# Banded attention with a gated feed-forward on one core: masks between the value tiles, last Q/K tokens third, global exponentials first, third batch by hardware DMA

## The chip, the core and the metric

The kernel runs on one core of one Trainium2 chip. The core has five engines with instruction streams of their own: TensorE (PE), VectorE (DVE), ScalarE (ACT), GpSimd (POOL) and SyncE (SP, which here only issues DMA transfers). Each engine takes its instructions strictly in the order in which the program gives them; semaphores hold an instruction until its inputs are there and its buffer is free. The metric is the device time of one execution in microseconds (us). Lower is better.

## The reference, cut to what matters

```python
B, H, S, D = 8, 8, 576, 64            # batch, heads, tokens, head size; 8 global tokens
scores = q @ k.T / sqrt(D)
mask = |i - j| <= 32  or  i is global  or  j is global
x = softmax(where(mask, scores, -1e9)) @ v            # then to (4608, 512): tokens x (heads * D)
g, val = x @ w_gate, x @ w_val                        # 512 -> 1536
ffn = (gelu(g) * val) @ w_out                         # 1536 -> 512
out = x + sigmoid(x @ w_res) * ffn
```

Inputs and outputs are fp32; the kernel multiplies in bf16 and accumulates in fp32.

## The kernel before

**Windows and chunks.** Each batch of 576 tokens is cut into 9 windows of 64 queries, each of which sees 128 keys around it. The 72 windows of the 8 batches are taken in 9 chunks of 8 windows (512 tokens): a chunk is the unit of the feed-forward part. `sc` holds the scores of four windows (a *quad*) and two heads; `weigh` (L456) takes the exponential into `pt` on ACT, and one multiplication by `maskw` per bank on DVE (L469) takes away what lies outside the band. So a quad has four exponentials and four masks, and a chunk has two quads. `values` (L484 to L504) makes a *value tile* of two windows: PE multiplies `pt` with the values into the psum tile `nd`, of which there is one buffer, and DVE divides (`rden`, `xtok`). Tiles 0 and 1 use quad 0, tiles 2 and 3 use quad 1. `turn_x` transposes the result into `xt`, by DMA for the first three tiles of chunks 2 to 8 and on PE otherwise.

**Global tokens.** Their Q, K and V rows are gathered by indirect DMA (`gather`, L285), four sets for the eight batches. `global_scores` (L404, L409) multiplies them with all keys and queries of a batch, `global_exp` (L416, L418, L420) takes the exponentials `ptg` and `gt` and masks the second, and `global_rows` (L426) makes the outputs of the global rows in `sn`, which shares the buffer of `nd`.

**Feed-forward.** For each of 12 slices j, `ffn_in` (L522 to L530) makes the gate and value products, GELU on ACT, and their product `ht` on DVE. `ffn_out` gives four jobs for each 128 tokens t: the residual gate (`r_ps` L539, tanh L542) and three *thirds* of the output product (`f_ps`, L549). The last third adds `prb` on DVE (L553), `ob` on POOL (L555) and the store on SP (L557). `prb` and `ob` have two buffers each.

**Order.** There is no scheduler: the order is written out by hand. While chunk c goes through `ffn_out`, the scores and values of chunk c+1 stand between its 16 jobs; a table `jobs` says what goes ahead of which. For chunks 1 to 7:

```python
jobs[0].append(lambda: global_exp(b, *held))
jobs[4].append(lambda: global_rows(b))
for quad in range(2):
    jobs[1 + 4 * quad].append(lambda quad=quad: scores(c + 1, quad))
for t in range(4):
    jobs[5 + 2 * t].append(lambda t=t: values(c + 1, t))
    jobs[7 + 2 * t].insert(0, lambda t=t: turn_x(c + 1, t))
```

The end of chunk 0 has an order of its own (L690 and after), since there batch 1 has just come in.

**Psum.** `psm` has four banks (products, part of the scores), `pss` two (the other scores, transposes), `psn` one double bank (`sg`, `sn`, `nd`).

**Loads.** The first two batches come as fp32 by hardware DMA on SP (`load_raw` L159, `load_vraw` L177), as do the weights in 20 pieces of 512 KB (`load_piece` L134). They land in staging room, part of which are buffers that are not yet in use, and are cast by POOL, DVE or ACT (`cast_pair` L253, `cast_v` L182, `cast_piece` L137). `q_st` and `k_st` hold Q and K of one batch in bf16 by tokens; `turn_pair` transposes them on PE for the first two batches, `turn_qk` (L398) by DMA for the others, whose loads (`load_qk` L91, `load_v` L99) are casting DMA transfers that POOL issues. `shift_v` copies the values shifted by 64 tokens from `ve` to `vo`.

Of the kernel before, what the change touches and what calls it, by code (L numbers as in the profile page):

```python
# [23 lines left out]
def kernel(  # L24
# [12 lines left out]
    nc = tc.nc  # L37
# [124 lines left out]
    for p in (0, 1, 2, 3, -1):  # L162
        load_raw(0, "k", p, nc.sync)
        if p == 0:
            nc.scalar.dma_start(gi8, bass.AP(tensor=g32.tensor, offset=g32.offset, ap=[[2, NG], [1, 2]]))
        load_raw(0, "q", p, nc.scalar if p in (0, 1) else nc.sync)
# [13 lines left out]
    def cast_v(b, c, copy):  # L180
        for p0, p1 in ((32, 64), (64, 128)) if c == 0 and b else ((0, 96 if c == 4 else 128),):
            copy(ve[b][p0:p1, c, :, 0:D], vplace[b][c][p0:p1, :].rearrange("p (h d) -> p h d", d=D))  # L182

# [275 lines left out]
    def scores(c, quad):  # L459
# [7 lines left out]
        for pp, u, sc in banks:  # L467
            mine = weigh(quad, pp, u, sc)
            nc.vector.tensor_tensor(mine, mine, view(maskw, 0, 128, 64 * i0, [[0, 2], [64, 4], [1, 64]]), ALU.mult)  # L469
# [94 lines left out]
    for p, by in ((0, (DVE, ACT)), (1, (DVE, ACT)), (2, (POOL, POOL)), (3, (POOL, POOL)), (-1, (POOL, ACT))):  # L564
        if p == 1:
            first_masks()
        for what, copy in zip("kq", by):
            cast_pair(0, p, what, copy)
        if p == 0:
            nc.scalar.activation(far, iota_f, ACTF.Square, bias=ngp, scale=1.0)  # L570
    for what in "kq":
        turn_pair(0, 0, what)
    hot_rows(0)
# [3 lines left out]
    first_scores(0, 0)  # L577
    for what in "kq":
        turn_pair(0, 2, what)
# [7 lines left out]
    for what in "kq":  # L587
        turn_pair(0, -1, what)
    sg, ss = global_scores(0)
    first_scores(0, 1)  # L590
    nc.vector.scalar_tensor_tensor(maskg, far, 1024.5, nong, ALU.is_gt, ALU.mult)
    fill(blk, 1.0, [([[-8, 16]], 1, 0, ALU.is_ge, 0.0), ([[8, 16]], -1, 7, ALU.is_ge, 0.0)])
    global_exp(0, sg, ss)
    nc.vector.tensor_tensor(diag, blk[:, 0:8], blk[:, 8:16], ALU.add)
# [31 lines left out]
    for c in range(NCH):  # L626
        b = c + 1
        if b < B and c:
            turn_qk(b)
            if c == 1:  # L630
# [3 lines left out]
            load_v(b)  # L634
        held = None
        for j in range(NFF):
            ffn_in(c, j)
            if c == 0:
# [14 lines left out]
                elif j == 5:  # L653
# [6 lines left out]
                    for n in (14, 15, 16, 17):  # L660
                        load_piece(n)
                    for n in (12, 13):
                        cast_piece(n, POOL)
                        load_piece(n + 6)
                    for c5 in range(5):
                        cast_v(1, c5, POOL)
                    for n in range(14, 20):
# [4 lines left out]
            elif b < B:  # L672
                if c == 1:
                    if j == 8:
                        double_qk(1, B // 2)
                    elif j == 9:
                        got = turn_globals(1, B // 2)
                        for what in "kq":
                            DVE(compact[what][:, 1:B // 2, :], got[what])
                        spread_v(1, B // 2)  # L680
# [10 lines left out]
        if c == 0:  # L691
            held = global_scores(1)
            work_f[0]()
            global_exp(1, *held)
            shift_v(1, nc.scalar)
            scores(1, 0)
            work_f[4]()
            scores(1, 1)
            work_f[8]()
            work_f[12]()  # L700
            global_rows(1)
            for i, n in enumerate((1, 5, 2, 6, 3, 7, 9, 10, 11, 13, 14, 15)):
                work_f[n]()
                if i < 4:
                    values(1, i)
                if 1 < i < 6:
                    turn_x(1, i - 2)
                if i == 3:
                    load_qk(2)
                    for what in "kqv":  # L710
                        gather(what, 1)
            continue
        jobs = {n: [] for n in range(16)}
        if c + 1 < NCH:
            if held is not None:
                jobs[0].append(lambda: global_exp(b, *held))
                jobs[4].append(lambda: global_rows(b))
            for quad in range(2):
                jobs[1 + 4 * quad].append(lambda quad=quad: scores(c + 1, quad))
            for t in range(4):  # L720
                jobs[5 + 2 * t].append(lambda t=t: values(c + 1, t))
                jobs[7 + 2 * t].insert(0, lambda t=t: turn_x(c + 1, t))
        for n in range(16):
# [32 lines left out]
```

## Time and profile before

| | |
|---|---|
| median of 9 runs | 425.27 us (424.11 to 426.23) |
| the profiled execution | 425.4 us; span from first to last instruction 423.7 us |
| busy, share of the span | PE 92%, DVE 48%, POOL 41%, ACT 40% |
| mean granted TensorE clock | 0.994 |
| start, to the first gate product of chunk 0 | 0 to 34.75 us |
| chunk 0, gate and value products | 34.75 to 59.69 us |
| chunk 0, output part (with batch 1's first scores) | 59.69 to 85.67 us |
| chunk 1 | 85.67 to 129.79 us |
| chunk 2 | 129.79 to 172.57 us |

Times in the table's lower half are positions in the profiled execution. An instruction's idle time is that of its engine just before it, and the arrow behind it names what ended that idle time. Where several things were waited for, only the one that came last is named. The clock row says at what share of full speed TensorE was let run.

### The profile page before, as it was taken

How to read it: one execution, taken by the hardware profiler on the slowest of the kernel's cores; microseconds unless marked ns; L12 is line 12 of the kernel's file. 1: busy time of each engine (PE TensorE's matmuls, PEld its weight loads, DVE VectorE, ACT ScalarE, POOL GpSimd, SP SyncE). 2: the span in 40 equal slices, each digit the busy share in tenths (PEclk: the TensorE clock that was granted, in tenths of full speed). 3: DMA queues.
4: the chain of work that ended last, by engine and by line, in shares of the span. 5: the costliest groups of instructions: out<-in, count | busy, mean ns of one | idle time of the engine just before them, and what ended most of it. 6: DMA issues, size and time to landing. Idle time of an engine off the chain costs nothing.

```text
span 423.7 us, 7941 instructions
## 1 busy us (share of the span) xinstructions
PE 388.4 (92%) x3084; PEld 203.9 (48%) x3136; DVE 203.0 (48%) x414; ACT 168.7 (40%) x279; POOL 172.9 (41%) x208
## 2 busy tenths in 40 slices
PE   3478979999989999999899999998999999989995
PEld 2354445544554455445544554455445544544442
DVE  6455635535663455346534654365435543463321
ACT  4555556023524362435243523352335233614320
POOL 7688769379316621644165316431600120012012
PEclk9999998999999999999999999999999999999999
DMA  8999979149937993799379926993592230031001
GB/s 245 236 389 336 236 262 137 57 115 129 156 86 102 173 108 80 103 152 135 76 102 157 135 76 96 170 127 74 93 140 53 70 68 0 2 89 51 0 26 75
DMA packets 151830, 52.10 MB, mean 123 GB/s; under 512 B 136368, under 2 KB 140976, under 8 KB 151792
## 3 DMA queue, kind: packets, MB, share of 16 engines
q0 software_dynamic: 84768, 11.02, 41.6%
q1 hardware_dynamic: 66304, 39.52, 39.9%
q10 hardware_dynamic: 720, 1.06, 0.9%
q8 instruction: 24, 0.39, 0.4%
q14 instruction: 14, 0.11, 0.1%
HBM read 39.19 MB, written 9.44 MB: 115 GB/s over the span
## 4 chain that ended last, share of the span: by engine, by line
PE 55%; issue 27%; POOL 5%; ACT 4%; DMA 4%; DVE 3%; POOLq 0%; ACTq 0%; DVEq 0%
PE v_ps L526 15%; PE g_ps L522 14%; PE f_ps L549 11%; PE r_ps L539 4%; POOL ob L555 4%; DMA ht<-in_q_dram 3%; PE nd L490 2%; ACT pt L456 2%; PE sg L404 2%; PE nd L484 1%; PE sn L426 1%; PE sc L449 1%; DVE xtok L504 1%; DMA out_dram<-ob 1%; PE ss L409 1%
## 5 line engine op out<-in xcount | busy, mean ns | idle before, releaser
L555 POOL TENSOR_TENSOR ob<-prb,xtok 128x512 f32<-128x512 f32 x36 | 41.5, 1153 | 201.6 <-DVE prb L553 201.6
L530 DVE SCALAR_TENSOR_TENSOR ht<-gsb,v_ps 128x512 bf16<-128x512 bf16 x108 | 74.0, 687 | 99.7 <-PE v_ps L526 93.1
L529 ACT ACTIVATE gsb<-g_ps 128x512 bf16<-128x512 f32 x108 | 64.4, 597 | 137.2 <-PE g_ps L522 126.7
L526 PE MATMUL v_ps<-xt,wv_t 128*128 128x512 bf16 x431 | 110.8, 379 | 1.4 <-DVE ht L530 0.9
L522 PE MATMUL g_ps<-xt,wg_t 128*128 128x512 bf16 x415 | 108.5, 379 | 1.2 <-ACT xt L515 0.7
L549 PE MATMUL f_ps<-wo_t,ht 128*128 128x512 bf16 x413 | 99.8, 379 | 0.9
L526 PEld LDWEIGHTS <-wv_t 128*128 128x128 bf16 x432 | 42.2, 98 | 52.1 <-issue 1.2
L522 PEld LDWEIGHTS <-wg_t 128*128 128x128 bf16 x432 | 42.0, 98 | 50.4 <-issue 0.8
L549 PEld LDWEIGHTS <-ht 128*128 128x128 bf16 x432 | 39.2, 98 | 39.8
L542 ACT ACTIVATE rsb<-r_ps 128x512 bf16<-128x512 f32 x36 | 21.5, 599 | 87.9 <-PE r_ps L539 86.7
L553 DVE SCALAR_TENSOR_TENSOR prb<-rsb,f_ps 128x512 f32<-128x512 bf16 x36 | 24.7, 687 | 32.1 <-PE f_ps L549 29.5
L456 ACT ACTIVATE pt<-sc 128x512 bf16<-128x512 f32 x72 | 37.4, 609 | 3.1 <-PE sc L449 3.0
L539 PE MATMUL r_ps<-wr_t,xt 128*128 128x512 bf16 x129 | 36.8, 388 | 0.7
L469 DVE TENSOR_TENSOR pt<-pt,maskw 128x512 bf16<-128x512 bf16 x64 | 27.8, 438 | 17.8 <-ACT pt L456 14.9
L91 POOL DMA_DIRECT2D q_st<-in_q_dram x30 | 25.4, 870 | 22.5 <-DMA qt<-q_st 22.5
L91 POOL DMA_DIRECT2D k_st<-in_k_dram x30 | 25.5, 878 | 5.3 <-DMA kt<-k_st 4.1
L99 POOL DMA_DIRECT2D ve<-in_v_dram x30 | 25.5, 866 | 0.0
L504 DVE TENSOR_TENSOR xtok<-nd,rden 128x512 bf16<-128x512 f32 x34 | 23.5, 691 | 1.3
L484 PE MATMUL nd<-vgs,gt 128*128 128x260 bf16 x80 | 15.0, 277 | 9.0 <-DVE xtok L504 6.6
L490 PEld LDWEIGHTS <-pt 128*128 128x128 bf16 x576 | 22.2, 97 | 1.1
L490 PE MATMUL nd<-ve,pt 128*128 128x65 bf16 x320 | 22.3, 193 | 0.0
L503 DVE RECIPROCAL rden<-nd 128x8 f32<-128x8 f32 x34 | 7.0, 206 | 29.5 <-PE nd L490 29.3
(134 smaller groups left out, 298.6 us busy)
## 6 DMA issues: line engine op xcount, KB each, us to landing
out_dram<-ob SPq DMA_DIRECT2D x36, 256.0 KB
vo<-ve SPq DMA_DIRECT2D x12, 260.0 KB
q_st<-in_q_dram POOLq DMA_DIRECT2D x24, 128.0 KB, 5.7
k_st<-in_k_dram POOLq DMA_DIRECT2D x24, 128.0 KB, 6.3
ve<-in_v_dram POOLq DMA_DIRECT2D x18, 128.0 KB, 5.9
wo_t<-in_k_dram SPq DMA_DIRECT2D x8, 256.0 KB
extra<-in_moe_w_gate_dram SPq DMA_DIRECT2D x4, 512.0 KB
extra<-in_moe_w_out_dram SPq DMA_DIRECT2D x4, 512.0 KB
```

What stands on the lines that cost most here:

```text
L91: nc.gpsimd.dma_start(dst[0:n, r, :].rearrange("p (h d) -> p h d", d=D), src[b].rearrange("h s d -> s h d")[128 * r:128 * r + n])
L456: nc.scalar.activation(mine, sc, ACTF.Exp, bias=0.0, scale=SCALE)
L469: nc.vector.tensor_tensor(mine, mine, view(maskw, 0, 128, 64 * i0, [[0, 2], [64, 4], [1, 64]]), ALU.mult)
L490: nc.tensor.matmul(nds[h // 4][:, VG * (h % 4):VG * (h % 4) + VG], view(pt, 0, 128, c0, [[1, 128]]), vw, start=False, stop=(h % 4 == 3 and ...
L504: nc.vector.tensor_tensor(xtok[c % 2][:, t, :].rearrange("p (a h d) -> p a h d", a=2, d=D), num[:, :, :, 0:D], view(rden, 0, 128, 0, [[4, ...
L522: nc.tensor.matmul(g_ps, wg_t[:, kk, 128 * j:128 * j + 128], x[:, kk, :], start=(kk == 0), stop=(kk == NKT - 1))
L526: nc.tensor.matmul(v_ps, wv_t[:, kk, 128 * j:128 * j + 128], x[:, kk, :], start=(kk == 0), stop=(kk == NKT - 1))
L529: nc.scalar.activation(gsb, g_ps, ACTF.Gelu, bias=0.0, scale=1.0)
L530: nc.vector.scalar_tensor_tensor(ht[:, j, :], gsb, 0.5, v_ps, ALU.mult, ALU.mult)
L539: nc.tensor.matmul(r_ps, xt[c % 2][:, kk, 128 * t:128 * t + 128], wr_t[:, kk, :], start=(kk == 0), stop=(kk == NKT - 1))
L549: nc.tensor.matmul(held["f"], ht[:, j, 128 * t:128 * t + 128], wo_t[:, j, :], start=(j == 0), stop=(j == NFF - 1))
L555: nc.gpsimd.tensor_tensor(ob, prb, xtok[c % 2][:, t, :], ALU.add)
```

## The change

Four things are moved or replaced; the computation stays.

1. `scores` no longer emits the masks; it returns a function that does. In chunks 1 to 7, value tile 0 stands ahead of the second quad's scores, two of that quad's masks stand behind tile 0 and two behind tile 1, and `global_rows` stands one job earlier. The end of chunk 0 is written out anew in the same manner.
2. At the start, the last 64 tokens of Q and K are loaded third and not last. Their casts, and that of `diag`, are on POOL. `hot_rows` and the transposes of the last tokens change places.
3. `global_exp` stands ahead of the next scores at the start, and ahead of the first residual gate at the end of chunk 0.
4. The third batch's Q and K come as fp32 by ten hardware DMA transfers on SP into staging room that the weight pieces have left, and POOL casts them (`load_second`, `cast_second`). `shift_v(1)` goes from ACT's queue to SP's, ahead of weight pieces 16 to 19. The gathers of set 1 go ahead of the casts of the output weights on POOL. The later sets' transposes are split between chunks 1 and 2, and `load_v` goes ahead of the gathers in chunk 1.

```diff
-    for p in (0, 1, 2, 3, -1):
+    for p in (0, 1, -1, 2, 3):
         load_raw(0, "k", p, nc.sync)
         if p == 0:
             nc.scalar.dma_start(gi8, bass.AP(tensor=g32.tensor, offset=g32.offset, ap=[[2, NG], [1, 2]]))
...
+
+
+    place2 = {"q": [vraw[:, r, :] for r in range(NQT)],
+              "k": [extra[:, r // 2, 512 * (r % 2):512 * (r % 2) + 512] for r in range(NQT)]}
+
+    def load_second(what):
+        for r in range(NQT):
+            n = min(128, S - 128 * r)
+            nc.sync.dma_start(place2[what][r][0:n, :].rearrange("p (h d) -> p h d", d=D),
+                              {"q": q, "k": k}[what][2].rearrange("h s d -> s h d")[128 * r:128 * r + n])
+
+    def cast_second(what, copy):
+        for r in range(NQT):
+            n = min(128, S - 128 * r)
+            copy({"q": q_st, "k": k_st}[what][0:n, r, :], place2[what][r][0:n, :])
...
-        for pp, u, sc in banks:
-            mine = weigh(quad, pp, u, sc)
-            nc.vector.tensor_tensor(mine, mine, view(maskw, 0, 128, 64 * i0, [[0, 2], [64, 4], [1, 64]]), ALU.mult)
+        mine = [weigh(quad, *which) for which in banks]
+
+        def mask(n0, n1):
+            for m in mine[n0:n1]:
+                nc.vector.tensor_tensor(m, m, view(maskw, 0, 128, 64 * i0, [[0, 2], [64, 4], [1, 64]]), ALU.mult)
+        return mask
...
-    for p, by in ((0, (DVE, ACT)), (1, (DVE, ACT)), (2, (POOL, POOL)), (3, (POOL, POOL)), (-1, (POOL, ACT))):
-        if p == 1:
-            first_masks()
-        for what, copy in zip("kq", by):
-            cast_pair(0, p, what, copy)
-        if p == 0:
-            nc.scalar.activation(far, iota_f, ACTF.Square, bias=ngp, scale=1.0)
+    def cast_raw(p, what, copy):
+        cast_pair(0, p, what, copy)
+
+    cast_raw(0, "k", DVE)
+    cast_raw(0, "q", ACT)
+    nc.scalar.activation(far, iota_f, ACTF.Square, bias=ngp, scale=1.0)
+    first_masks()
+    cast_raw(1, "k", DVE)
     for what in "kq":
         turn_pair(0, 0, what)
-    hot_rows(0)
+    cast_raw(1, "q", ACT)
+    for p in (-1, 2, 3):
+        for what in "kq":
+            cast_raw(p, what, POOL)
+    fill(blk, 1.0, [([[-8, 16]], 1, 0, ALU.is_ge, 0.0), ([[8, 16]], -1, 7, ALU.is_ge, 0.0)])
+    nc.gpsimd.tensor_tensor(diag, blk[:, 0:8], blk[:, 8:16], ALU.add)
     for what in "kq":
         turn_pair(0, 1, what)
     other_masks()
     first_scores(0, 0)
+    for what in "kq":
+        turn_pair(0, -1, what)
     for what in "kq":
         turn_pair(0, 2, what)
     double_qk(0, 1)
@@ -584,14 +610,11 @@
     spread_qk(0, got, 0, {"k": DVE, "q": ACT})
     for what in "kq":
         DVE(compact[what][:, 0:1, :], got[what])
-    for what in "kq":
-        turn_pair(0, -1, what)
     sg, ss = global_scores(0)
+    nc.vector.scalar_tensor_tensor(maskg, far, 1024.5, nong, ALU.is_gt, ALU.mult)
+    global_exp(0, sg, ss)
     first_scores(0, 1)
-    nc.vector.scalar_tensor_tensor(maskg, far, 1024.5, nong, ALU.is_gt, ALU.mult)
-    fill(blk, 1.0, [([[-8, 16]], 1, 0, ALU.is_ge, 0.0), ([[8, 16]], -1, 7, ALU.is_ge, 0.0)])
-    global_exp(0, sg, ss)
-    nc.vector.tensor_tensor(diag, blk[:, 0:8], blk[:, 8:16], ALU.add)
+    hot_rows(0)
...
             turn_qk(b)
+            load_v(b)
             if c == 1:
                 for n in range(2, B // 2):
                     for what in "kqv":
                         gather(what, n)
-            load_v(b)
...
                     load_vraw(1)
-                    for n in (14, 15, 16, 17):
+                    for n in (14, 15):
                         load_piece(n)
                     for n in (12, 13):
                         cast_piece(n, POOL)
-                        load_piece(n + 6)
                     for c5 in range(5):
                         cast_v(1, c5, POOL)
+                    shift_v(1)
+                    for n in range(16, 20):
+                        load_piece(n)
+                    for what in "kqv":
+                        gather(what, 1)
                     for n in range(14, 20):
                         cast_piece(n, POOL)
                 if j > 6:
                     for what in "kq":
-                if c == 1:
+                if c in (1, 2):
+                    n0, n1 = ((1, 2), (2, B // 2))[c - 1]
                     if j == 8:
-                        double_qk(1, B // 2)
+                        double_qk(n0, n1)
                     elif j == 9:
-                        got = turn_globals(1, B // 2)
+                        got = turn_globals(n0, n1)
                         for what in "kq":
-                            DVE(compact[what][:, 1:B // 2, :], got[what])
-                        spread_v(1, B // 2)
+                            DVE(compact[what][:, n0:n1, :], got[what])
+                        spread_v(n0, n1)
...
         if c == 0:
-            held = global_scores(1)
+            global_exp(1, *global_scores(1))
             work_f[0]()
-            global_exp(1, *held)
-            shift_v(1, nc.scalar)
-            scores(1, 0)
+            scores(1, 0)(0, 4)
             work_f[4]()
-            scores(1, 1)
             work_f[8]()
+            mask = scores(1, 1)
             work_f[12]()
             global_rows(1)
-            for i, n in enumerate((1, 5, 2, 6, 3, 7, 9, 10, 11, 13, 14, 15)):
+            for what in "kq":
+                load_second(what)
+            for what in "kq":
+                cast_second(what, POOL)
+            work_f[1]()
+            values(1, 0)
+            mask(0, 2)
+            work_f[5]()
+            values(1, 1)
+            mask(2, 4)
+            work_f[2]()
+            turn_x(1, 0)
+            work_f[6]()
+            values(1, 2)
+            turn_x(1, 1)
+            work_f[3]()
+            values(1, 3)
+            work_f[7]()
+            turn_x(1, 2)
+            work_f[9]()
+            work_f[10]()
+            turn_x(1, 3)
+            for n in (11, 13, 14, 15):
                 work_f[n]()
-                if i < 4:
-                    values(1, i)
-                if 1 < i < 6:
-                    turn_x(1, i - 2)
-                if i == 3:
-                    load_qk(2)
-                    for what in "kqv":
-                        gather(what, 1)
             continue
         jobs = {n: [] for n in range(16)}
         if c + 1 < NCH:
             if held is not None:
                 jobs[0].append(lambda: global_exp(b, *held))
-                jobs[4].append(lambda: global_rows(b))
-            for quad in range(2):
-                jobs[1 + 4 * quad].append(lambda quad=quad: scores(c + 1, quad))
+                jobs[3].append(lambda: global_rows(b))
+            held_mask = {}
+
+            def half(quad):
+                held_mask[quad] = scores(c + 1, quad)
+
+            jobs[1] += [lambda: half(0), lambda: held_mask[0](0, 4)]
             for t in range(4):
                 jobs[5 + 2 * t].append(lambda t=t: values(c + 1, t))
                 jobs[7 + 2 * t].insert(0, lambda t=t: turn_x(c + 1, t))
+            jobs[5].append(lambda: half(1))
+            jobs[6].append(lambda: held_mask[1](0, 2))
+            jobs[7].append(lambda: held_mask[1](2, 4))
```

## The prediction

> **What bounds the kernel now.** I read the page first (its busy line and its clock row), then the list of who waited for whom on TensorE, then the timeline around each long wait, stretch by stretch. TensorE is busy for 92% of the span, no other engine above 48%, so time is to be had only where PE waits or runs at a low clock. PE's list of waits (engine line waited for: us in total, times, longest):
>
> ```profile
> PE nd L484 <- DVE xtok L504: 6.6, 7, 1.2
> PE sc L449 <- ACT qt L391: 4.7, 2, 3.8
> PE sc L449 <- ACT ptg L416: 2.3, 1, 2.3
> PE sn L426 <- ACT gt L418: 1.1, 1, 1.1
> PE nd L484 <- DVE vgs L429: 1.1, 1, 1.1
> PE nd L484 <- DVE rden L503: 1.0, 1, 1.0
> ```
>
> The change touches all six rows. Row 1 is one wait in each of the seven steady chunks 1 to 7. The timeline of chunk 1 shows its cause (start, length, engine, line, [idle before <- releaser]):
>
> ```profile
> 116.75 1.90 DVE L469 TENSOR_TENSOR pt<-pt,maskw 128x512 bf16<-128x512 bf16 x4 [1.28 <-ACT pt L456]
> 118.67 0.21 DVE L503 RECIPROCAL rden<-nd 128x8 f32<-128x8 f32 x1
> 118.92 0.69 DVE L504 TENSOR_TENSOR xtok<-nd,rden 128x512 bf16<-128x512 f32 x1
> 119.67 0.40 PE L484 MATMUL nd<-vgs,gt 128*128 128x260 bf16 x2 [0.96 <-DVE xtok L504]
> ```
>
> Value tile 0 is done on PE at 117.03, but its division stands on DVE behind four masks that nobody needs until tile 2. The only nd buffer stays full, and tile 1 waits 0.96. Row 2 is the start:
>
> ```profile
> 13.10 0.62 ACT L250 CAST q_st<-ht 128x512 bf16<-128x512 f32 x1 [4.17 <-DMA ht<-in_q_dram]
> 13.63 0.58 ACT L391 COPY qt<-tq 128x512 bf16<-128x512 bf16 x1
> 14.26 0.40 PE L449 MATMUL sc<-qt,kt 64*128 64x64 bf16 x8 [3.81 <-ACT qt L391]
> ```
>
> ACT waits 4.17 for the last tokens of Q, and the copy that the first scores need stands behind that wait. Row 3 is the middle (end of chunk 0), and the clock behind it (stretch, its length, then busy PE, PEld, DVE, ACT, POOL, PEclk, DMA share, GB/s):
>
> ```profile
> 61.35 1.28 ACT L416 ACT_TABLE_LOAD   x1
> 63.13 0.69 PE L449 MATMUL sc<-qt,kt 64*128 64x64 bf16 x31 [2.29 <-ACT ptg L416]
> ...
> 64.00:66.00 2.00, 2.00 (x22) 0.73 (x22) 1.64 (x5) 2.00 (x5) 2.00 (x3) 0.50 1.25 108
> 66.00:68.00 2.00, 1.95 (x29) 1.09 (x25) 1.31 (x4) 2.00 (x5) 2.00 (x4) 0.76 2.14 143
> 68.00:70.00 2.00, 2.00 (x15) 1.36 (x14) 0.89 (x3) 1.98 (x4) 2.00 (x4) 1.00 2.21 139
> ```
>
> **Part 1, masks between the value tiles (chunks 1 to 7).** The built order puts value tile 0 ahead of the second score set, two masks after its division, and two after tile 1's. From the end of tile 0 to tile 1, PE now has the scores (0.6) and two thirds (1.73), 2.3 in all; DVE needs 0.1 + 0.21 + 0.69 = about 1.0 to free nd. The wait goes whole: -6.6. What is late next is tile 2, which needs masks 3 and 4. Counted from the end of tile 1: DVE divides (1.0) and masks (0.95), done at 1.95; PE has a third and a gate (1.73), then two small products and four heads (0.47), so it reads the last-masked heads at 2.2. Margin 0.25: tight but free. The exponentials behind those masks end some 2.1 after the scores, before tile 1 ends. `global_rows` a third earlier needs only the exponentials that ended at 109.94 in this chunk. The prb of t1 goes behind two masks (0.95 later); its psum bank is next wanted four allocations on, so nobody waits.
>
> **Part 2, the start.** K and Q of the last tokens (128 KB each) are loaded third and cast on POOL, so ACT's order is now: cast of Q pair 1 (landed 8.31, until 8.93), its transpose copy (until 10.0), exponentials. PE's bias products end at 10.4, so the first scores start there, not at 14.26. The bytes ahead of V are the same, so the piece that is last, now Q pair 3, lands where the last tokens did, about 13.1 (an estimate from that row). Then POOL's cast 0.61, four transposes 0.43, ACT copy 0.6, one tg transpose behind that copy: the global scores start at 15.15, before at 19.92: 4.8 earlier. The global exponentials no longer stand behind a score set: ACT from 17.85 does ptg 0.45, gt 0.65, pt 1.08, hot 0.67, vo 1.05, pt 1.08, vo 1.06, pt 1.08 = 7.1 and ends at 25.0 (before 29.23). Value tile 2 needs that last pt: 25.0 against 30.80, 5.8 earlier; from it to the first gate product it stays 3.95. I take the middle of 4.8 and 5.8: -5.3. POOL's one more cast and diag (two small operations) end before V's first chunk at 14.4, give or take 0.3; V's casts are paced by landing (19.12 for the last), so the weight casts from 21.84 stay. Weights and second-batch casts (36.8 to 44.9) are needed from 43 on even at the earlier time.
>
> **Part 3, the middle.** From the first gate (59.69) to chunk 1's first product (85.67) are 25.98. The work at full clock: 4 gates and 12 thirds at 0.86 = 13.8, scores 2 x 0.64, sn 1.12, four value tiles at 0.93, four transposes at 0.22: 20.8. The other 5.2 are 2.29 for ptg, 0.96 and 0.23 for nd, and 1.7 of half clock (3.4 at 0.50). Now the table load and both global exponentials stand ahead of the gate's tanh: the last Q copy ends (58.64) 1.05 before the gate starts; load 1.28 and ptg 0.44 bring ptg's end to 0.7 after that start, while PE is in the gate (0.86). New waits: the second score set needs psum from the first set's exponentials, which end at 4.0 while PE is there at 3.2 (0.55, and 0.3 for gate 3's bank); nd about 0.3. So 5.2 - 1.15 = -4.0.
>
> The clock term is a choice. The trace: after idle of 2.29 PE ran at 0.50 for about 3.4. [...] The row stands directly behind the gap, so I take -4.0.
>
> **Part 4, third batch by hardware DMA.** SP gains ten loads (2.36 MB, 256-byte runs) behind the weight pieces; POOL loses ten DMA issues (8.6) and gains ten casts of 0.61, ahead of the four ob. Nearest row for the rate: the second batch's V, same layout, 1.18 MB between 47.2 and 52.8, so 210 GB/s: 11.2. The shift of V moved to SP waits there for V's casts (53.44), and pieces 16 to 19 stand behind it, issued at 54.7 instead of 50.1 and landed near 62.5. Loads land until 73.7, casts end at 74.3. The first prb is ready near 69.5, so the first ob waits 4.8; prb has two buffers, so DVE waits 1.8 at the third prb and is done at 77.3, while its next product is due at 78.3. Cost 0, with 1 us of cover. The gathers (3 x 1.25) now stand before the output-weight casts on POOL: these end at 59.4, 61.4 and 63.9 in pairs; PE wants the pairs at 61.1, 64.8 and 67.9. Cost 0, cover 1.7. If DVE's masks here run beside POOL's casts, 0.69 (the gt mask at 25.4) instead of 0.46 each bounds the cost at 8 x 0.23 = 1.8; most is off PE's path, I take 0.
>
> **Part 5, split of the later globals.** Chunk 2 gains about 1.6 of DVE copies. In chunk 1 a larger pile of them (104.95 to 107.75) made PE wait for nothing: 0. Chunk 1's other wait (v_ps for ht, 0.9, ACT late once) has no cause in the trace that I can name; I leave it.
>
> **Sum.** 6.6 + 5.3 + 4.0 = 15.9. The profiled execution took 425.4 (span 423.7 and 1.7 around it), 0.1 above the median: 409.5 on it, 409.4 for the median.
>
> **Rivals.** (a) Likeliest, 0.75: all three parts come, each within its own error: start 4 to 6, middle 2.3 to 4.5, steady 5.5 to 6.9, so 407.5 to 413.5. (b) 0.17: the cover of part 4 or part 1 is gone. At the start five V loads took 8.69 to issue, 1.74 each; at that rate casts end near 78.5 and PE loses 3 to 4; or the 0.25 margin at tile 2 fails, 0.3 to 0.5 in each of seven chunks. Either gives about 412.5 to 416. For: POOL and DVE are strict queues. Against: DMA is nearly idle there (20 GB/s from 60 to 62). (c) 0.04, slower: the loads back up on SP. One V load there took 3.7 to issue. Ten at that price from 58.3 end at 95, every ob stands behind them on POOL, and PE stops in chunk 1 for 20 and restarts cold: about 431. It turns slower from 3.2 per load. [...] (d) 0.04, no difference or the gain is spent elsewhere: tile 1 still waits and the start is paced by V and weights, not by Q; about 422 to 426. Against: V is cast by 19.73, and the weights by 36.87 are needed in thirds from 29 on.
>
> **Numbers.** Prediction 409.4; range 406 to 416, which is (a), (b) and unknown costs on the good side (a wait of 0.9 in chunk 1 gone, a start of 6). A measurement of this kernel tells about 0.2% from no change (0.85 us). Faster 0.94, same 0.02, slower 0.04.
>
> **What would show it.** nd <- xtok gone from PE's waits; first scores near 10.4, global scores near 15, chunk 0's first product near 29.4; no 0.50 in the clock row in the middle, and 22 from the first gate to chunk 1; ob of chunk 0 starting near 74. Wrong if nd waits for masks, if chunk 0 starts after 32, or if PE waits for prb or ht early in chunk 1.

## The result, and the profile after

The changed kernel takes 409.5 us (median of 10 runs, 408.16 to 415.56), against 425.27 before: ratio 0.965 [0.9623, 0.9677], here and below with its 95% interval. It is taken over the single runs, so it is not the quotient of the medians; one run, 415.56, fell in a slower state of the chip and is left out of it. Two later comparisons on other occasions gave 0.9689 [0.9647, 0.9732] and 0.9682 [0.9639, 0.9724]. The profiled execution took 411.92 (span 410.2 and 1.7 around it), 2.4 above its median, so the account below is made against 425.4 - 411.9 = 13.5. All line numbers from here on are those of the changed kernel unless a run is an edit of the kernel before.

TensorE's largest waits (engine line waited for: us in total, times, longest) between 50 and 112 us; from there to the end its list, which leaves out the smallest, is empty:

```profile
PE g_ps L540 <- DVE prb L571: 3.5, 1, 3.5
PE f_ps L567 <- POOL wo_t L137: 1.7, 2, 1.3
PE tg L364 <- DVE kgd L354: 1.2, 1, 1.2
PE sg L419 <- ACT qt L404: 0.3, 1, 0.3
PE nd L502 <- DVE xtok L522: 0.2, 1, 0.2
```

All the rows shown of before are gone or nearly so: nd for xtok fell from 6.6 to 0.2, the waits for `qt` at the start and for `ptg` in the middle from 7.0 to parts of a us. Three new rows stand in their place, and all three lie between the output part of chunk 0 and the end of chunk 1. The same stretches of the two profiled executions, with what the prediction gave each:

| stretch | before | after | difference | predicted |
|---|---|---|---|---|
| start, to chunk 0's first product | 34.75 | 26.06 | -8.7 | -5.3 |
| chunk 0, products | 24.94 | 24.94 | 0 | 0 |
| chunk 0, output part | 25.98 | 23.39 | -2.6 | -4.0 |
| chunk 1 | 44.12 | 48.53 | +4.4 | -1.0 |
| chunk 2 to the end of the span | 293.91 | 287.28 | -6.6 | -5.6 |
| sum | | | -13.5 | -15.9 |

The total came within 2.4, but large errors of opposite sign lie in it: the start gave 3.4 more than predicted, and chunk 1 lost 5.4 against its forecast.

**The start.** First scores and global scores (start, length, engine, line, [idle before <- releaser]):

```profile
7.31 0.62 ACT L268 CAST q_st<-ht 128x512 bf16<-128x512 f32 x1
8.62 0.59 ACT L406 COPY qt<-tq 128x512 bf16<-128x512 bf16 x1 [0.70 <-issue]
9.37 0.61 PE L464 MATMUL sc<-qt,kt 64*128 64x64 bf16 x16
...
14.10 1.15 PE L419 MATMUL sg<-qt,kgz 128*128 128x288 bf16 x8 [0.42 <-DVE kgz L373]
15.78 0.44 ACT L431 ACTIVATE ptg<-ss 128x320 bf16<-128x320 f32 x1 [1.69 <-PE ss L424]
...
21.30 1.07 ACT L471 ACTIVATE pt<-sc 128x512 bf16<-128x512 f32 x2
```

The cast of the last tokens of Q has left ACT's queue, and the copy that the first scores need follows the second cast at once. The eight global score products took 2.16 before and take 1.15 here, although the clock row shows 1.00 in both places. That is not a sure part of the change: in e10 and e12 below, whose start is the same and where TensorE has no idle time above 1.2 between 6 and 16 us, they took 2.13 again.

```profile
15.38 2.13 PE L419 MATMUL sg<-qt,kgz 128*128 128x288 bf16 x8
```

That row is e10's. What sets their speed is not shown.

**The middle.** Table load, global exponentials and scores:

```profile
49.97 1.28 ACT L431 ACT_TABLE_LOAD   x1
51.00 1.02 PE L557 MATMUL r_ps<-wr_t,xt 128*128 128x512 bf16 x3
51.27 0.44 ACT L431 ACTIVATE ptg<-ss 128x320 bf16<-128x320 f32 x1
51.95 0.64 PE L464 MATMUL sc<-qt,kt 64*128 64x64 bf16 x32
```

The scores follow the gate with no wait, where 2.29 stood before.

**Between the value tiles.** Chunk 1's output part again, tile 0's division and tiles 1 and 2:

```profile
110.60 0.21 DVE L521 RECIPROCAL rden<-nd 128x8 f32<-128x8 f32 x1 [0.82 <-PE nd L508]
110.84 0.69 DVE L522 TENSOR_TENSOR xtok<-nd,rden 128x512 bf16<-128x512 f32 x1
111.56 0.91 DVE L486 TENSOR_TENSOR pt<-pt,maskw 128x512 bf16<-128x512 bf16 x2
112.80 0.39 PE L502 MATMUL nd<-vgs,gt 128*128 128x260 bf16 x2
...
114.56 0.75 DVE L486 TENSOR_TENSOR pt<-pt,maskw 128x512 bf16<-128x512 bf16 x2
115.24 0.39 PE L502 MATMUL nd<-vgs,gt 128*128 128x260 bf16 x2
```

The division stands ahead of the masks, and neither tile 1 nor tile 2 has an idle time in brackets.

**Where time was lost.** In chunk 0's output part, the output product waits for the second pair of weight casts, and POOL for the landing of its second piece:

```profile
62.62 1.04 POOL L137 CAST wo_t<-vraw 128x1024 bf16<-128x1024 f32 x1 [2.32 <-DMA vraw<-in_moe_w_out_dram]
63.71 0.59 PE L567 MATMUL f_ps<-wo_t,ht 128*128 128x512 bf16 x2 [1.28 <-POOL wo_t L137]
```

The other 0.39 of that wait, at 58.73, are for the first pair, which POOL casts behind the gathers. SP issues the shift of V, four weight pieces and then the ten loads (start, length of the issues, queue):

```profile
52.96 0.55 SPq L103 DMA_DIRECT2D vo<-ve  x1
53.57 0.58 SPq L104 DMA_DIRECT2D vo<-ve  x1
54.19 1.28 SPq L134 DMA_DIRECT2D vraw<-in_moe_w_out_dram  x2
55.52 1.31 SPq L134 DMA_DIRECT2D extra<-in_moe_w_out_dram  x2
57.72 9.55 SPq L191 DMA_DIRECT2D extra<-in_k_dram  x5
67.32 6.19 SPq L191 DMA_DIRECT2D vraw<-in_q_dram  x5
```

The pieces are issued 4 us later than before (50.12 to 52.61). POOL casts the third batch's Q until its last load lands, then comes `ob`; DVE's third `prb` waits for it, and PE for that:

```profile
76.69 1.17 POOL L197 CAST q_st<-vraw 128x512 bf16<-128x512 f32 x2 [0.92 <-DMA vraw<-in_q_dram]
77.83 2.26 POOL L573 TENSOR_TENSOR ob<-prb,xtok 128x512 f32<-128x512 f32 x2
79.00 0.69 DVE L571 SCALAR_TENSOR_TENSOR prb<-rsb,f_ps 128x512 f32<-128x512 bf16 x1 [7.44 <-POOL ob L573]
79.75 1.02 PE L540 MATMUL g_ps<-xt,wg_t 128*128 128x512 bf16 x4 [3.46 <-DVE prb L571]
```

Behind that gap TensorE's clock falls (stretch, its length, busy PE, PEld, DVE, ACT, POOL, PEclk, DMA share, GB/s):

```profile
80.00:82.00 2.00, 1.78 (x6) 0.65 (x6) 1.28 (x2) 0.60 (x1) 0.91 (x2) 0.66 0.63 244
82.00:84.00 2.00, 1.91 (x5) 0.73 (x5) 0.69 (x1) 0.00 (x0) 1.83 (x3) 0.50 0.34 131
84.00:86.00 2.00, 2.00 (x11) 0.88 (x9) 0.69 (x1) 0.60 (x1) 2.00 (x3) 0.98 0.51 140
```

Chunk 1 is 3.46 (wait) + 1.7 (half clock: 2 x 0.34 + 2 x 0.50 = 1.7) + 1.25 (the wait for `kgd`) = 6.4 longer than the 42.1 that are left, and 42.1 is what other runs below show for it.

### The profile page after: what moved, and what is told of

Same layout as the page of the kernel before. It is cut to its first block, busy times and chain, and to the rows that moved or that the text cites. A ratio compares the mean times of both kernels' runs of the same rounds, so it can differ in the third digit from the quotient of the medians.

```text
span 410.2 us, 7953 instructions
## 1 busy us (share of the span) xinstructions
PE 386.2 (94%) x3084; PEld 204.4 (50%) x3136; DVE 202.0 (49%) x418; ACT 169.2 (41%) x278; POOL 171.3 (42%) x210
## 4 chain that ended last, share of the span: by engine, by line
PE 59%; issue 17%; DMA 12%; SPq 6%; POOL 4%; DVE 1%; POOLq 0%; ACTq 0%
PE v_ps L544 15%; PE g_ps L540 15%; PE f_ps L567 14%; PE r_ps L557 5%; DMA extra<-in_moe_w_gate_dram 4%; SPq L177 4%; DMA vraw<-in_q_dram 3%; POOL ob L573 3%; PE nd L508 3%; DMA extra<-in_moe_w_out_dram 2%; PE sc L464 2%; PE sn L441 2%; PE nd L502 1%; PE sg L419 1%; DMA vo<-in_v_dram 1%
## 5 line engine op out<-in xcount | busy, mean ns | idle before, releaser
L486 DVE TENSOR_TENSOR pt<-pt,maskw 128x512 bf16<-128x512 bf16 x64 | 26.9, 434 | 8.6 <-ACT pt L471 6.5
L91 POOL DMA_DIRECT2D q_st<-in_q_dram x25 | 21.2, 865 | 20.9 <-DMA qt<-q_st 20.9
L522 DVE TENSOR_TENSOR xtok<-nd,rden 128x512 bf16<-128x512 f32 x34 | 23.5, 692 | 1.3
L91 POOL DMA_DIRECT2D k_st<-in_k_dram x25 | 21.2, 878 | 3.4 <-DMA kt<-k_st 2.6
L557 PEld LDWEIGHTS <-xt 128*128 128x128 bf16 x144 | 13.4, 97 | 15.1
```

Source lines behind the costliest of these rows:

```text
L91: nc.gpsimd.dma_start(dst[0:n, r, :].rearrange("p (h d) -> p h d", d=D), src[b].rearrange("h s d -> s h d")[128 * r:128 * r + n])
L486: nc.vector.tensor_tensor(m, m, view(maskw, 0, 128, 64 * i0, [[0, 2], [64, 4], [1, 64]]), ALU.mult)
L557: nc.tensor.matmul(r_ps, xt[c % 2][:, kk, 128 * t:128 * t + 128], wr_t[:, kk, :], start=(kk == 0), stop=(kk == NKT - 1))
```

## The experiments

Each part alone on the kernel before, then the changed kernel with one thing taken back. Runs e1 to e4 were compared with one set of runs of the kernel before (median 423.42), e5 to e8 with another (424.17), e9 to e12 with a third (423.68). Ratios are to the kernel before. The position of the first product in each chunk, in each profiled execution:

| run | chunk 0 | chunk 1 | chunk 2 | ratio |
|---|---|---|---|---|
| before | 34.75 | 85.67 | 129.79 | 1 |
| after | 26.06 | 74.39 | 122.92 | 0.965 [0.9623, 0.9677] |
| e1, masks only | 35.18 | 85.40 | 127.33 | 0.9803 [0.9765, 0.9841] |
| e2, start only | 25.90 | 75.52 | 124.29 | 0.9948 [0.9921, 0.9975] |
| e3, middle exponentials only | 33.85 | 81.43 | 124.96 | 0.9949 [0.9922, 0.9975] |
| e4, third batch's casts late | 27.70 | 76.46 | 118.91 | 0.9639 [0.9593, 0.9685] |
| e5, after again | 27.10 | 74.95 | 123.11 | 0.9689 [0.9647, 0.9732] |
| e6, pieces first | 27.83 | 79.82 | 121.90 | 0.9618 [0.9588, 0.9648] |
| e7, third batch by POOL | 25.93 | 73.47 | 117.23 | 0.9622 [0.9588, 0.9655] |
| e8, last tokens last | 29.61 | 79.00 | 121.08 | 0.9655 [0.9625, 0.9684] |
| e9, after a third time | 26.17 | 74.84 | 123.07 | 0.9682 [0.9639, 0.9724] |
| e10, part 4 undone | 28.70 | 75.58 | 122.80 | 0.9707 [0.9663, 0.975] |
| e11, three moves | 28.43 | 79.17 | 121.18 | 0.9645 [0.9605, 0.9684] |
| e12, three moves, POOL's loads | 27.26 | 77.36 | 119.50 | 0.9635 [0.959, 0.9679] |

**e1, the masks between the value tiles alone** (the kernel before with part 1's order of chunks 1 to 7):

```diff
-            for quad in range(2):
-                jobs[1 + 4 * quad].append(lambda quad=quad: scores(c + 1, quad))
+            jobs[1] += [lambda: half(0), lambda: held_mask[0](0, 4)]
...
+            jobs[5].append(lambda: half(1))
+            jobs[6].append(lambda: held_mask[1](0, 2))
+            jobs[7].append(lambda: held_mask[1](2, 4))
```

> The kernel before with the steady part alone: in chunks 1 to 7 value tile 0 ahead of the second score set, its masks two behind tile 0 and two behind tile 1, global rows a job earlier. The end of chunk 0 and the start stay. Theory: PE's seven waits for nd (6.6 us in all) go and nothing takes their place: about 418.7, which is 6.6 below the kernel before. Rival: tile 2 now waits for the last two masks, or DVE's later prb for a psum bank: 0 to 3 below, 422 or more, and PE's list of waits names pt or prb.

Measured: 414.75 us, 8.7 below the kernel before's 423.42. In its profile nd waits for xtok nowhere in chunks 1 to 8. From chunk 2 to the end it takes 414.6 - 127.3 = 287.3, the same as the changed kernel: 6.6 less than before, of which the list of waits had named 5.7; the other 0.9 stood in no wait of the list, and where they were is not shown. Chunk 1 is 2.2 shorter: 1.0 for nd and 0.9 for `ht`, which did not come this time. So part 1 is worth more than half of the whole gain, and it is the part that was kept in full.

**e2, the start alone** (the kernel before with part 2 and the start's half of part 3):

```diff
-    for p in (0, 1, 2, 3, -1):
+    for p in (0, 1, -1, 2, 3):
         load_raw(0, "k", p, nc.sync)
...
+    for p in (-1, 2, 3):
+        for what in "kq":
+            cast_raw(p, what, POOL)
```

> The kernel before with the start alone changed: last tokens third, their casts and diag on POOL, global exponentials ahead of the next scores. In the changed kernel chunk 0's first gate product came 8.7 earlier, where 5.3 was forecast. Theory: the start passes on whole, since the weights are there in time: 8 to 8.7 below the kernel before, about 417. Rival: what comes behind is paced by loads (output weights, second batch's V, third batch's Q and K issued by POOL), so that half of it is waited away before chunk 1: 4 to 5 below, about 421. [...]

Measured: 420.52, only 2.9 below by the medians (5.5 between the two profiled executions), although chunk 0 begins 8.85 earlier in its profile. All of that is still there when chunk 1 begins (75.52 against 85.67); the loss comes in chunk 1. Its waits there (L522 and L553 are g_ps and prb, L409 the global scores):

```profile
PE g_ps L522 <- DVE prb L553: 2.1, 1, 2.1
PE ss L409 <- DMA kt<-k_st: 1.4, 2, 1.1
```

and POOL's row shows why: the first ob stands behind the issues of the third batch's loads and the gathers.

```profile
76.63 0.96 POOL L285 DMA_INDIRECT vgf<-in_v_dram,idx  x1 [0.30 <-issue]
77.61 2.27 POOL L555 TENSOR_TENSOR ob<-prb,xtok 128x512 f32<-128x512 f32 x2
```

With the clock's drop behind the wait for prb (0.56 from 80 to 82, 0.59 from 82 to 84), chunk 1 takes 48.77 instead of 44.12. The earlier start runs into a supply that does not come earlier: POOL begins the third batch's issues at 65.14, behind the casts of the output weights, which wait for their landing; in the kernel before it began them at 62.83.

**e3, the global exponentials ahead of the first gate, alone:**

```diff
+            global_exp(1, *held)
             work_f[0]()
-            global_exp(1, *held)
```

> The kernel before with one line moved: at the end of chunk 0 the two global exponentials stand ahead of the first residual gate. Theory: the 2.29 wait goes and with it the half clock behind it (1.7); the second score set then waits about 1.3 for the exponentials of the first: 2.4 to 3 below the kernel before, about 422.6, and no 0.50 in the clock row from 60 to 70. Rival, the clock drop is not due to this gap: the row keeps 0.50 for 3.4 us, and the time is only about 1 below, 424.2.

Measured: 420.5, 2.9 below. In its profile the output part of chunk 0 takes 22.65 (58.78 to 81.43) instead of 25.98, so 3.3 less. The wait for `ptg` is gone, and with it the half clock:

```profile
60.00:62.00 2.00, 1.52 (x32) 0.75 (x24) 1.04 (x2) 1.57 (x4) 1.70 (x2) 1.00 0.85 243
62.00:64.00 2.00, 1.52 (x36) 1.00 (x35) 1.58 (x4) 2.00 (x5) 0.44 (x2) 1.00 0.66 173
```

**e4, the third batch's casts behind chunk 0's four ob** (the changed kernel otherwise):

```diff
-            for what in "kq":
-                cast_second(what, POOL)
...
             for n in (11, 13, 14, 15):
                 work_f[n]()
+            for what in "qk":
+                cast_second(what, POOL)
```

> The changed kernel with POOL's ten casts of the third batch's Q and K behind the four ob of chunk 0, Q first. Theory: in the changed kernel these casts end at 77.9, the ob stand behind them, and PE waits 3.5 for prb early in chunk 1, with half clock behind it: both go, so 3.5 to 5 below the changed kernel, about 405. Rival: the transposes of the third batch, which wait for the casts, come too late for the global scores at the end of chunk 1's products, so the gain turns into a wait there: 408 to 411.

Measured: 406.63, ratio 0.9639 [0.9593, 0.9685]. The wait for prb is gone, the clock is 1.00 there, and chunk 1 takes 42.45. POOL's ob now wait for DVE and not the reverse:

```profile
70.21 1.15 POOL L573 TENSOR_TENSOR ob<-prb,xtok 128x512 f32<-128x512 f32 x1 [1.63 <-DVE prb L571]
```

The price is half a us later on, in the list of waits:

```profile
PE ss L424 <- DMA kt<-k_st: 0.5, 1, 0.5
```

So it is the place of the casts in POOL's queue that made PE stop. The waits for `wo_t` (2.0) stay. That the whole kernel gains by it is not shown: the changed kernel did not run beside e4, and its own intervals on the other occasions overlap e4's.

**e5 and e9, the changed kernel again**, as measures on the chips of the later runs:

> The changed kernel once more, as the measure for the other three runs on this chip. Expected as before: 0.965 of the kernel before, so about 409 where that takes 424. Its own waits: 3.5 in g_ps for prb and 1.7 in f_ps for wo_t, if they belong to the order and not to one execution; if they come from where the transfers happened to land, they change by a us or more here.

> The changed kernel once more, as the measure for the other three runs on this chip. Expected 0.965 to 0.969 of the kernel before, with the waits for prb (3 to 3.5) and kgd (1.2) in chunk 1 as in both profiles so far.

Measured: 411.76 and 411.0. The wait for prb is there both times (3.2), as is the one before the transposes of the globals (1.25 and 1.1); that for `wo_t` is not listed in e5 and is 1.9 in e9. In e5 the casts are not earlier (the second pair ends at 63.51), but PE stops 1.22 at 57.03 for a reason the trace does not name and comes to them at 63.84; in e9 1.35 of the 1.9 are for the first pair. So this wait depends on how PE's arrival and the casts lie to each other. Chunk 0 begins at 26.06, 27.10 and 26.17 in the three profiles, but chunk 2 at 122.92, 123.11 and 123.07: a start that is 1 us later changes nothing by then.

**e6, weight pieces 16 to 19 ahead of the shift of V, and the casts late:**

```diff
-                    for n in (14, 15):
+                    for n in (14, 15, 16, 17):
                         load_piece(n)
                     for n in (12, 13):
                         cast_piece(n, POOL)
+                        load_piece(n + 6)
...
                     shift_v(1)
-                    for n in range(16, 20):
-                        load_piece(n)
```

> The changed kernel with the third batch's casts behind chunk 0's four ob, and with weight pieces 16 to 19 issued where the kernel before issued them, ahead of the shift of V on SP. Theory: f_ps waits for wo_t (1.7 to 2.0) because those pieces stand behind the shift on SP and share the DMA engines with the K loads. Then these waits go, and with the prb wait gone as well the time is 5 to 6 below the changed kernel's profiled sum, about 2 below the version with the late casts alone: ratio to before 0.957 to 0.960. Rival: POOL's order, not the landing, makes wo_t late (the gathers, 3.75, ahead of the casts): then a wait for wo_t of 1 or more stays and the ratio is 0.962 to 0.965.

Measured: 408.12, ratio 0.9618. The wait for `wo_t` is gone as the theory said, but a new one of nearly twice its size is there, which neither side had named: the shifted values now land behind the pieces.

```profile
66.55 0.20 PE L508 MATMUL nd<-vo,pt 128*128 128x65 bf16 x1 [3.11 <-DMA vo<-ve]
```

and the clock behind that gap:

```profile
68.00:70.00 2.00, 2.00 (x9) 1.03 (x8) 1.21 (x4) 0.00 (x0) 0.00 (x0) 0.50 0.98 214
```

Chunk 1 then takes 42.08. What is put first on SP made the other late here. In e10 below the pieces are ahead as well, but the shift is on ACT's queue and no loads stand behind it on SP: tile 0 reads `vo` at 63.98 without a wait. Which of the two it takes is not separated.

**e7, the third batch by POOL's casting transfers again** (the main step of part 4 undone):

```diff
-            for what in "kq":
-                load_second(what)
-            for what in "kq":
-                cast_second(what, POOL)
+            load_qk(2)
```

> The changed kernel with the third batch's Q and K loaded by POOL's casting transfers, as in the kernel before, at the same place in the order (part 4's main step undone). Theory: part 4 is what lets the earlier start be kept. POOL issues ten transfers (8.6) ahead of the first ob, which ends near 75 and not 77.8, so the prb wait shrinks to about 1, but the transfers land late, and the third batch's transposes and with them chunk 1's global scores wait for kt: 1.5 to 3 there, as in the run with the start alone. In all within 1 of the changed kernel, 0.5 slower by choice. Rival: the part is worth its whole start: 3 or more slower, ratio to before above 0.971. Other rival: it costs, and the kernel is 1 to 3 faster without it, 0.958 to 0.962.

Measured: 407.99 against 411.76 for e5 on the same chip; the six runs of each, resampled, give 0.992 [0.988, 0.997]. That is the second rival: the hardware transfers cost time here. The profiled execution starts as the changed kernel's does (25.93) and reaches chunk 2 at 117.23, 5.7 earlier. POOL's queue:

```profile
69.60 4.26 POOL L91 DMA_DIRECT2D k_st<-in_k_dram  x5
73.77 2.38 POOL L573 TENSOR_TENSOR ob<-prb,xtok 128x512 f32<-128x512 f32 x2
```

and the waits of chunk 1 that are left (in the middle, 0.8 for the output weights are left too, in two waits of 0.4):

```profile
PE ss L424 <- DMA kt<-k_st: 1.1, 1, 1.1
PE g_ps L540 <- DVE prb L571: 0.5, 1, 0.5
```

POOL is done with its ten issues at 73.77 and need not wait for a landing; in the changed kernel its casts wait for the last load and end at 77.83.

**e8, the last tokens last again**, but cast on POOL and with the global exponentials first:

```diff
-    for p in (0, 1, -1, 2, 3):
+    for p in (0, 1, 2, 3, -1):
         load_raw(0, "k", p, nc.sync)
...
-    for p in (-1, 2, 3):
+    for p in (2, 3, -1):
         for what in "kq":
             cast_raw(p, what, POOL)
```

> The changed kernel with the last 64 tokens of Q and K loaded, cast and transposed last again, but their casts still on POOL and the global exponentials still first. Theory: the gain at the start is that ACT no longer waits for a landing in front of the copy that the first scores need; which pair is loaded last matters little, since the bytes are the same. First product of chunk 0 within 0.7 of the changed kernel's, the time within 0.2%. Rival: the load order matters, since the last tokens are only half a transfer and four fewer transposes: then the start is 1 to 2 later, and the time 0.2 to 0.5% above the changed kernel.

Measured: 409.93 against 411.76. Chunk 0 begins at 29.61. Part of that is the landing of Q's second pair, which was cast at 8.46 here and at 7.31 in the changed kernel; in e4, where it was cast as late (8.54), the start is 27.70, 1.9 earlier. Of these, 0.96 are there when the global scores begin (16.14 against 15.18), which leaves about 1 for the order of loading, the low end of the rival; the other 0.96 are these products taking 2.10 instead of 1.14, as they also do in e10 and e12 with the changed kernel's start. On the time neither expectation holds: a start that is 3.5 later than the changed kernel's costs nothing that can be seen. In e8 the casts end at 78.67, hardly later than at 77.83, and chunk 1 begins at 79.00, so nothing waits; chunk 2 begins 1.8 earlier. The last 3.5 of the start only turn into a wait for prb.

**e10, part 4 undone but for the split of the later globals:**

```diff
-            for what in "kq":
-                load_second(what)
-            for what in "kq":
-                cast_second(what, POOL)
+            load_qk(2)
+            for what in "kqv":
+                gather(what, 1)
...
             global_exp(1, *global_scores(1))
             work_f[0]()
+            shift_v(1, nc.scalar)
```

> The changed kernel with all of part 4 but the split of the later globals undone: third batch by POOL's transfers, the gathers of set 1 behind them, the shift of V on ACT's queue, weight pieces 16 to 19 issued ahead. Theory: part 4 as a whole costs time once parts 1 to 3 are there. No wait for wo_t; POOL starts its issues near 61 and is done with loads and gathers near 74, so prb waits 1 or less; the third batch's K lands some 3 earlier than in the run with POOL's loads alone, so the wait for kt goes. Ratio to before 0.955 to 0.962, 3 to 5 below the changed kernel. Rival: the gathers ahead of the ob cost what they save, or V's shift on ACT's queue is late: a wait of 2 or more for prb or vo, and the ratio equals the changed kernel's.

Measured: 411.18 against 411.0 for e9: the rival. The three gathers (1.0 and 0.3 each) are back ahead of the ob, which starts at 77.34, as late as with the hardware loads; prb waits 1.8 and `kt` 1.6. As a whole, what was undone of part 4 is worth nothing that can be told either way; within it the hardware loads with their casts lose (e7). The gathers' place seems to gain, by the traces alone: in e7, where they stay early, the ob start at 73.77.

**e11 and e12, three moves together**: pieces first, the shift of V on ACT's queue as before, and the casts late (e11) or POOL's transfers (e12).

```diff
             global_exp(1, *global_scores(1))
             work_f[0]()
+            shift_v(1, nc.scalar)
```

> The changed kernel with three moves: the third batch's casts behind chunk 0's four ob, pieces 16 to 19 ahead, and the shift of V on ACT's queue as in the kernel before. Theory: this takes away the wait for prb, the wait for wo_t and the wait of 3.1 for vo that the second move alone brought, so only the load of K and Q is left of part 4: chunk 0's output part 22 to 22.5, chunk 1 42 to 42.5, ratio to before 0.954 to 0.959. Rival: the shift on ACT's queue shares the DMA engines with the pieces and lands as late: vo waits 1 or more, and the ratio stays at 0.961 to 0.964.

> The same as the run before it, but with the third batch loaded by POOL's casting transfers ahead of the ob (gathers of set 1 still ahead of the output weights' casts). It sets POOL's transfers against the hardware ones with all else equal. Theory: POOL's ten issues (8.6) start at 62 to 63 and end near 71.5, before the first prb would stall anything: no prb wait, K lands in time for chunk 1's global scores or 0.5 late. Within 0.2% of the run with hardware transfers. Rival: hardware transfers are worth having: 0.3% or more faster there.

Measured: 409.19 and 408.61, not the 404 to 406 that e11's theory gave. The waits for prb, `wo_t` and `vo` are gone in both, and chunk 1 takes 42.0 and 42.1, but a new wait opens in the middle, where PE wants the second score set's psum and ACT's exponentials are late; the clock falls behind it. The timeline of e11, and its clock row:

```profile
59.00 1.08 ACT L471 ACTIVATE pt<-sc 128x512 bf16<-128x512 f32 x2 [2.15 <-PE sc L464]
59.65 0.19 PE L464 MATMUL sc<-qt,kt 64*128 64x64 bf16 x1 [1.94 <-ACT pt L471]
```

```profile
60.00:62.00 2.00, 1.77 (x19) 0.91 (x19) 2.00 (x1) 2.00 (x6) 2.00 (x3) 0.64 1.05 244
```

The scores that the row names had ended a us earlier, so what held ACT for 2.15 is not in the trace. The two transfers on its queue are not enough to explain it: e10 has them too and no such stop, and e5, which has them on SP, stops at the same scores (the 1.22 at 57.03). A delay of ACT without a named cause also comes in chunk 1 (2.20 at 95.78 in the changed kernel, just ahead of the wait for `kgd`; 2.96 at 97.20 before). In e5 and e9 it is DVE that is late ahead of that wait, so its cause stays open. The two ways of loading the third batch differ by less than can be told, as expected of e12.

e6 and e7 gain most over the changed kernel on the same chip: 0.993 [0.989, 0.998] and 0.992 [0.988, 0.997] of e5. They beat both kernels, and e7 does it with less code.

## Why the prediction was right, and where it was not

The forecast of 409.4 met the median, and the three parts that it named came, but that it met so closely was luck. Alone, the parts are worth 8.7, 2.9 and 2.9 (e1, e2, e3), 14.5 in sum, where the forecast had 6.6, 5.3 and 4.0; together, a surplus at the start paid for a loss in chunk 1. That loss is one of the signs that the prediction itself had named for being wrong: PE waits for prb early in chunk 1. By its steps:

- **Part 1 (-6.6): right in mechanism, 1 to 2 short.** Tiles 1 and 2 start without a wait; the margin of 0.25 at tile 2 held (masks done at 115.3, tile 2 at 115.24 with its last-masked heads after that). The stretch from chunk 2 on alone gave 6.6, with chunk 1 on top; e1 gave 8.7. The term was mis-sized because only waits on the list were counted.
- **Part 2 (-5.3): right in mechanism, 3.4 short.** The forecast chain had ACT at `ptg` at 17.85 and the value tile 2 at 25.0. Measured: `ptg` at 15.78 and tile 2 at 22.11; from there to the first gate product it is 3.95, as said. The 2.1 at `ptg` are 1.05 because the global scores began at 14.10, not 15.15, and 1.0 because those products took 1.15 and not 2.16, which was chance at least in part (2.13 in e10 and e12). Another 0.8 are ACT's chain: it was summed to 7.1, took 6.6, and tile 2 started 0.26 before its end. The last 0.5 are the forecast's own choice of the middle between 4.8 and 5.8. With the same start in ten profiles, chunk 0 began at 25.90 to 28.70, always before the forecast 29.4. But e8 shows that the surplus earned nothing: it is given back at chunk 1.
- **Part 3 (-4.0): 1.4 short, for a reason outside it.** The `ptg` wait and the half clock went; e3 shows them as 3.3 by themselves. The new waits, booked at 1.15, came to 0.22 for the psum bank and 0.2 for nd. What took the gain is f_ps waiting for `wo_t`, 1.7. That is part 4's step "cost 0, cover 1.7". The second pair of casts, for which PE waited 1.28, ends at 63.66, not at 61.4, and PE came for its second piece at 62.43, where the forecast had 64.8 for the pair, since the start had run ahead. The K loads behind the pieces are not what makes the pieces late, or only in part: e7 has no such loads on SP, and there the second pair ends at 62.74 and PE still waits 0.8. e6 removes the wait by moving the pieces.
- **Part 4 (cost 0, cover 1): the step that failed.** Pieces and loads were timed at 54.7 to 73.7, 19.0 in all, by adding two terms. Measured: 54.19 to about 76.6, where POOL's wait for the last load ends, 22.4. The sum had no term for the shift of V just ahead, 0.52 MB, which at its own 210 GB/s would be 2.5 (an estimate; no run separates it). The casts ended at 77.86, not at 74.3, and PE came to the psum bank that prb frees at 76.29, not at 78.3, so both ends of the cover of 1 moved. PE lost 3.46, close to the 3 to 4 that rival (b) gave; the half clock behind it, 1.7, and the 1.25 at `kgd` were not in that rival. e4 (casts behind ob) and e7 (no hardware loads) remove the wait for prb, each by its own way. The wait for `kgd` is not there in them either.
- **Part 5 (0).** The transposes that it split are those before which PE waits 1.25 for `kgd` in chunk 1. The split alone does not bring that wait: e4, e6, e7, e8, e10 and e11 keep the split and have none. Its cause stays open.
- **The clock.** Taking half clock for a 2.29 gap was right for this profile and not a rule: in e2 the same gap of 2.29, which ends at 54.28, had none behind it (1.00 from 54 to 62). Without its clock term part 3 would be -2.3, the low end that rival (a) gives the middle. Gaps of 1.58 (e10, at 101.73), 1.85 (e12), 1.94 (e11) and 2.29 (before, e1) had some 3.4 at half rate behind them, while those of 2.29 (e2) and 1.80 (e10, at 79.27) had none. What makes the difference is not shown.

The rivals: (a) gave the time, but not by its own account: its start was 4 to 6 and the measured one is 8.7. (b) named what happened in chunk 1. Both hold in part, since the start's surplus paid for (b). (c) did not come: ten loads took 15.7 on SP to issue, 1.6 each, below the 3.2 at which it would have turned.

## What to carry to other kernels

A stage that starts earlier is worth only what the next supply allows: before booking a gain at the front, follow the loads and the strict queues that come after it, and ask which of them start earlier too (here 8.85 at the start alone were worth 2.9). A cast that is put ahead of an urgent operation on the same engine inherits the landing time of its load (here the casts put the first ob at 77.83; with them behind it, in e4, it began at 70.21); put it behind, or issue a transfer there that waits for nothing. A stop of TensorE of 2 to 3 us should be booked at its length and up to 1.7 more for the clock behind it: here stops of 2.13 (e2), 2.29 (before) and 3.11 (e6) had 1.7 behind them, one of 2.29 (e2) had none.

## What the runs showed of the hardware that was not expected

The half clock behind a gap does not follow from the gap's length alone: three gaps of 0.96, 0.32 and 0.35 within 2.7 us (e8, at 56.67 to 58.33) were followed by it, and in one execution, e10, a gap of 1.80 was not and one of 1.58 was. The clock behind e8's gaps:

```profile
60.00:62.00 2.00, 2.00 (x35) 1.03 (x33) 2.00 (x4) 1.84 (x5) 1.06 (x1) 0.50 1.00 340
```

and e10's: the clock behind the gap of 1.80, which ends at 79.27, then the gap of 1.58 and the clock behind it:

```profile
80.00:82.00 2.00, 1.92 (x10) 0.80 (x9) 1.42 (x3) 0.60 (x1) 1.28 (x2) 1.00 0.38 146
...
101.73 0.26 PE L424 MATMUL ss<-qgz,kt 128*128 128x16 bf16 x4 [1.58 <-DMA kt<-k_st]
...
104.00:106.00 2.00, 2.00 (x6) 0.74 (x5) 1.70 (x4) 1.49 (x4) 0.00 (x0) 0.50 2.42 154
```

The other surprise is how much the same start differs between executions: the second pair of Q was cast between 7.30 (e12) and 8.58 (e11) in kernels with the same code up to there, the eight global score products took between 1.14 (e5) and 2.13 (e10, e12), and chunk 0 began between 25.90 (e2) and 28.70 (e10). A difference of 1 or 2 us at the start of one profile is therefore no sign of an edit's effect.
